# Attention and feed-forward on one core: values of batch 0 on ScalarE's DMA queue, the first weight's transfers ahead of the second's, other constants for the planned order

## The chip, the cores and the metric

The kernel runs on one core of a Trainium2 chip. Its engines are TensorE (PE, matrix products), VectorE (DVE), ScalarE (ACT), GpSimd (POOL) and SyncE (SP, which here only issues DMAs). The metric is the device time of one execution in microseconds (us). The kernel before took 361.05 us, the median of three runs (359.9 to 361.69).

## The reference

Causal attention with 16 extra "beacon" keys and values in front, for 8 batches, 8 heads, 576 rows and 64 dimensions; then a feed-forward layer with an ELU between its two products, on 4608 tokens of 512 features with 2048 hidden ones.

```python
k_all = concatenate([beacon_k, k], axis=2)
v_all = concatenate([beacon_v, v], axis=2)
scores = (1 / sqrt(D)) * matmul(q, k_all^T)
scores = where(causal, -1e9, scores)
a = exp(scores - scores.max(-1)); a /= a.sum(-1) + 1e-9
attn = matmul(a, v_all)
x = attn.transpose(0, 2, 1, 3).reshape(B * S, H * D)
h = x @ w_in
g = where(h > 0, h, exp(min(h, 0)) - 1)
out = g @ w_out
```

## The kernel before

The heads of a batch are worked on in four pairs (`HP = 4`; pair n is batch n // 4, pair n % 4 in it). One pair goes through these steps:

- load of k and q (`load_pair`, L310) into one `st` buffer of four, cast to bf16 (`cast_pair`, L317 and L319), transposes on PE and copies out of PSUM to `kT` and `qT` (`do_T2` and `do_copy2` for batch 0, L394 to L411; `do_T`, `do_kT`, `do_qT` for batches 1 and 2, L384 to L426). From batch 3 on (`PE_B = 3`) tokens are loaded whole (`load_tok`) and transposed by DMA (`turn_tok`, L349).
- scores (`do_SC`, L435), exponentials on ACT (`do_exp`, L444), causal masks on POOL (`do_mask`, L450), the product with the values (`do_AV`, L469; the value tile has a column of ones, so the sum of the row comes with it), the division (`do_norm`, L484 and L485, DVE), and the transposes of the result into `xT` (`do_xT`, `do_xcopy`, L495 and L506, or by DMA, `turn_x`, L355). Batch 0 does this in three ranges of query rows, and a range needs the chunks of values that its rows can see.

The values of a batch come in five chunks of 128 keys (`load_v`, L361 for the 16 beacon rows of the first chunk and L365). Chunk jc of batch b has the name v(5b + jc): v0 to v4 are batch 0, v5 to v9 batch 1. They land in four buffers called `vst`, which the beacon keys (b0, b1, b2) use too, and are cast by DVE (`cast_v`, L369).

The feed-forward layer takes the tokens in tiles: 128, 128, 256 and then 512 rows. `do_mm1` (L522) makes hidden values in PSUM, `do_e` (L528, ACT) their exponential, `do_clamp` (L532, POOL) and `do_join` (L541, DVE) the ELU, `do_mm2` (L549) the second product, `do_osb` and `do_store` (L555, L559) the output. Its two weights come in four chunks each on POOL's queue (`load_w`, L376).

Nothing here is in the order in which it is written. Each step is added to a `Plan` with an engine, a key, an estimated duration, the steps it depends on and the buffers it takes and gives; `Plan.run` plays this through as a list scheduler while the program is built: whenever an engine is free it takes the ready step with the smallest key, and the instructions are then written out in that order, which each engine follows on the chip. On PE a step whose key is more than 16 above the smallest one not yet done is not taken. While the plan's time is below 30 and PE has nothing ready, it writes `spare` matmuls (`do_fill`, L272). The keys come from the constants at L563 to L577:

- `SHIFT` and `AT`: a step of batch b has the key `32 * (b - 1) + 8 * (hp + AT[i]) + SHIFT[b]`; `AT0` gives the keys of batch 0's scores, for three ranges and four pairs. `URGE` is taken off the keys of copies and divisions.
- `PACES` and `LAG`: the keys of the feed-forward tiles.
- `FIRST`: the order of the first loads, ahead of every other load. k0, q0 and b0 come before them.
- `W_AFTER`: for each of the four chunks of the two weights, the number of the mark after which it is issued. The marks are the masks of batches 0 and 1 and the first beacon cast, sorted by key; negative numbers mean the first mark.
- `ON_ACT`: whether token loads of k, of q, and value loads (of batches 3 and up) are issued by ACT; otherwise SP issues them. `ON_POOL` says which engine casts pair n (0 DVE, 1 POOL, 2 ACT), `TOK` the same for tokens, `Q_ON_ACT` and `X_ON_ACT` which batch's copies ACT does.

Loads on the same queue are issued in the order of their keys. ACT's loads stand in the same instruction stream as its exponentials.

Of the kernel before, what the change touches and what calls it, by code (L numbers as in the profile page):

```python
# [26 lines left out]
class Plan:  # L27
# [5 lines left out]
    def add(self, *args, **kw):  # L33
        op = Op(*args, **kw)
        self.ops.append(op)
        return op
# [102 lines left out]
def kernel(  # L139
# [87 lines left out]
    PE_B = 3  # L227
# [32 lines left out]
    with tc.tile_pool(name="psum", bufs=1, space=bass.MemoryType.PSUM) as psum:  # L260
# [21 lines left out]
        def load(key, dur, fn, deps=(), take=(), issue=0.47, units=1, on="SP"):  # L282
            ring = ["ring" + on] * units
            issue = add(on, key, issue, fn, deps=deps, take=take + ring)
            issues[on].append(issue)
            if "vst" not in take:
                issues["st"].append(issue)
            return add("DMA", key, dur, None, deps=[issue], lat=2.0, give=ring, queue=0 if on == "SP" else 2, parts=2 * units)

        issues = {"SP": [], "ACT": [], "st": []}  # L290
        add("SP", -1e6, 0.8, None)
        add("PE", -1e6, 1.3, None, mode=0)
# [264 lines left out]
        def do_store(tt, t4):  # L557
# [2 lines left out]

        SHIFT = [26.52, -13.69, -7.54, -1.34, 6.61, 17.9, 20.31, 13.93]  # L563
        AT = [-45.47, -1.07, -1.14, -0.54, -0.28, 0.56, 0.84, -22.77]
        AT0 = [[-37.75, -28.54, -33.52, -38.24], [-24.55, -26.86, -32.24, -21.75], [-25.0, -22.71, -32.03, -23.64]]
        PACES = [(-23.75, 5.53, 18.69, 9.14), (4.36, -4.25, 29.71, 6.23), (-11.12, 1.43, 43.67, -1.88), (36.29, 0.26, 8.05, 3.71), (81.1, 1.29, 17.28, 1.76), (112.87, 2.15, 30.1, 2.15)]
        W_AFTER = [[-11.34, -130.29, -36.3, -85.47], [23.62, 2.53, 18.3, 19.29]]
        DMA_AT = [-71.28, -109.08, 210.39]
        TOK = ("010110", "101001", "110100", "111111", "101001")
        ON_POOL = "11000121"  # L570
        X_ON_ACT = "00"
        LAG = 20.54
        URGE = 125.33
        Q_ON_ACT = "11001010"
        FIRST = (
            "v1 k2 q2 q3 k1 v2 q4 k3 q1 v0 v4 v3 k4 q6 b1 q5 v6 q7 k6 k5 v5 v8 k7 v9 v7 ").split()
        ON_ACT = "011"  # L577

        def place(b, a):
            return 32 * (b - 1) + 8 * a + SHIFT[b]  # L580

# [6 lines left out]
        def load_key(name, key):  # L588
            return ["k0", "q0", "b0"].index(name) - 900 if name in ("k0", "q0", "b0") else FIRST.index(name) - 200 if name in FIRST else key
# [3 lines left out]
        def plan_loads(n):  # L593
# [8 lines left out]
            for is_k in (True, False):  # L602
# [3 lines left out]
                "0": ("DVE", 0.9, nc.vector), "1": ("POOL", 1.23, nc.gpsimd), "2": ("ACT", 1.35, nc.scalar),  # L606
            }[ON_POOL[n] if n < len(ON_POOL) else "1"]
            qk_in[n] = add(
                eng, place(b, hp + AT[0]), dur, partial(cast_pair, n, on), deps=gots + [last_T.get(("pair", n - 2))], take=["sb"], give=["st"])

        last_T = {}

        def plan_v(b):
            for jc in range(NKC):
                key = load_key(f"v{NKC * b + jc}", place(b - 1, 1.8 + 0.4 * jc))
                on, eng = QUEUES[ON_ACT[2] == "1" and b >= PE_B]
                got = load(key, 1.22, partial(load_v, b, jc, eng), take=["vst"], issue=1.2 if jc == 0 else 0.6, units=8, on=on)
                v_cast[b, jc] = add(
                    "DVE", place(b, -0.7 + 0.16 * jc), 0.56, partial(cast_v, b, jc),
                    deps=[got] + last_AV.get(b - 2, []), give=["vst"])  # L620

        def plan_w(which, f4):
            after = marks[max(0, min(len(marks) - 1, round(W_AFTER[which][f4])))]
            got = add("POOL", after.key + 0.01, 0.8, partial(load_w, which, f4), deps=[after])
            got = add("DMA", 0, 3.2, None, deps=[got], lat=2.0, queue=1, parts=8)
            w_at.update({(which, 4 * f4 + c): got for c in range(4)})
# [3 lines left out]
        ring4, QUEUES = ["ringSP"] * 4, (("SP", nc.sync), ("ACT", nc.scalar))  # L630

        def plan_tok(b):
            turned[b] = []
            for is_k in (True, False):
                for c in range(0, NKC, 2):
                    m = min(2, NKC - c)
                    i = (0 if is_k else 0.5) + c // 2
                    on, eng = QUEUES[ON_ACT[not is_k] == "1"]
                    gots = [load(place(b, 0) - 30 + i + 0.01 * j, 1.22, partial(load_tok, b, is_k, c + j, eng), units=8, on=on,
                                 take=["st"] if j == 0 else [], issue=1.2 if is_k and c + j == 0 else 0.65) for j in range(m)]  # L640
                    on_dve = TOK[b - PE_B][3 * (not is_k) + c // 2] == "0"
                    cast = add("DVE" if on_dve else "POOL", place(b, DMA_AT[0]) + i, 0.36 * m if on_dve else 0.53 * m,
                               partial(cast_tok, b, is_k, c, m, nc.vector if on_dve else nc.gpsimd),
                               deps=gots, take=["sb"], give=["st"])
                    for j in range(m):
                        s = add("SP", place(b, DMA_AT[1]) + i, 1.25, partial(turn_tok, b, is_k, c + j),
                                deps=[cast] + last_SC.get(b - 2, []), take=ring4)
                        turned[b].append(add("DMA", place(b, DMA_AT[1]) + i, 0.6, None, deps=[s],
                                             give=ring4 + (["sb"] if j == m - 1 else []), lat=1.9, parts=8))

        def plan_T2(n, key):
            b, hp = divmod(n, HP)
            T = last_T["pair", n] = add(
                "PE", key, 0.56, partial(do_T2, n), deps=[qk_in[n], bk_in[b]], take=["ff", "ff"], give=["sb"],
                mode=0, lat=0.19)
            last_T.setdefault(b, []).append(T)
            kA = add("DVE", key + 0.4 - URGE, 0.47, partial(do_copy2, n, 0, 0, nc.vector), deps=[T])
            qB = add("ACT", key + 0.4 - URGE, 0.4, partial(do_copy2, n, 1, 1, nc.scalar), deps=[T])
            qA = add("ACT", key + 0.5 - URGE, 0.45, partial(do_copy2, n, 1, 0, nc.scalar), deps=[kA])
            kB = add("DVE", key + 0.5 - URGE, 0.57, partial(do_copy2, n, 0, 1, nc.vector), deps=[qB])  # L660
            add("NONE", key, 0.0, None, deps=[kA, qA], give=["ff"], lat=0.0)
            add("NONE", key, 0.0, None, deps=[kB, qB], give=["ff"], lat=0.0)
            return [kA, kB, qA, qB]

        def plan_T(n, key):
# [5 lines left out]
            last_T["pair", n] = T  # L671
            kT = add("DVE", key + 0.4 - URGE, 0.92, partial(do_kT, n), deps=[T, last_kq.get(n - NKQ)])
            if Q_ON_ACT[b] == "1":
                qT = add("ACT", key + 0.4 - URGE, 0.7, partial(do_qT, n, nc.scalar), deps=[kT, last_kq.get(n - NKQ)])
            else:
# [4 lines left out]
        def plan_pair(n):  # L680
            b, hp = divmod(n, HP)
            at = lambda a: place(b, hp + a)
            key = AT0[0][hp] - 4 if b == 0 else at(AT[1])
            ready = plan_T2(n, key) if b == 0 else plan_T(n, key) if b < PE_B else turned[b]
            masked = {}
            SC = None
            steps = [((0,), AT0[0][hp]), ((1, 2), AT0[1][hp]), ((3,), AT0[2][hp])] if b == 0 else \
                [((0, 1), at(AT[2])), ((2, 3), at(AT[3]))]
            for units, key in steps:
# [19 lines left out]
            for r, groups in enumerate([(0,), (1,), (2,)] if b == 0 else [(0,), (1, 2)]):  # L709
                key = AT0[r][hp] + 2.4 if b == 0 else at(AT[4 + r])  # L710
                us = [u for g in groups for u in CUT.of_range[g]]
# [9 lines left out]
                if b >= XB:  # L721
                    for blk in blks:
                        part.setdefault(blk, []).append(normed[-1])
                    if hp == HP - 1:
                        for blk in blks:
                            s = add("SP", at(AT[7]), 1.25, partial(turn_x, b, blk), deps=part.pop(blk), take=ring4)
                            done = add("DMA", at(AT[7]), 0.6, None, deps=[s], give=ring4, lat=1.9, parts=8)
                            last_X.setdefault(b, []).append(done)
# [13 lines left out]
                normed = []  # L742
                on_act = X_ON_ACT[b] == "1"
                done = add("ACT" if on_act else "DVE", key - URGE, 0.17 + 0.00104 * w if on_act else 0.15 + w / 1920,
# [6 lines left out]
        def plan_tile(p):  # L751
            lo, hi = TILES[p]
            base, pitch1, start2, pitch2 = PACES[p] if p < len(PACES) else (32 * (p - 2) + LAG,) + PACES[-1][1:]
            xs = []
# [45 lines left out]
        for b in range(B):  # L800
            plan_v(b)
            if b >= PE_B:
                plan_tok(b)
            for hp in range(HP):
                if b < PE_B:
                    plan_loads(b * HP + hp)
                plan_pair(b * HP + hp)
# [40 lines left out]
```

## Time and profile before

The page of the profiled execution gives the span from the first to the last instruction and the busy time of each engine.

| what | us |
|---|---|
| median of three runs | 361.05 |
| the profiled execution | 360.17 |
| its span | 358.5 |
| PE busy, `spare` among it | 344.4 |
| `spare` matmuls (117) | 19.1 |
| L522 and L549, the feed-forward products | 143.1 and 143.8 |
| scores and A·V (L435, L469) | 35.2 and 40.1 |
| DVE, ACT, POOL busy | 205.1, 192.7, 183.8 |

The granted clock of PE is at full speed nearly throughout (mean 0.998). The DMA engines are at nine tenths or more in most of the slices up to 250 us. In the listing of waits, a line "A <- B: t, n, longest" says that A's engine stood t us in n waits which B ended. In the timeline each row is a start, a length, the engine, the line, the operation and its tiles; "q" behind an engine's name is its queue of DMA issues. In the table of stretches, busy time is the time in which at least one instruction of the engine was under way.

### The profile page before, as it was taken

To read this page: it belongs to the slowest core of one execution; us is meant where nothing else is said; L and a number is where in the kernel's file an instruction comes from. 1 tells how busy PE (TensorE), PEld (TensorE's weight loads), DVE (VectorE), ACT (ScalarE), POOL (GpSimd) and SP (SyncE) were. 2 spreads that over 40 slices of the span, in tenths; PEclk is the share of its full clock that TensorE was granted. 3 is DMA by queue.
4 is the path that set the end of the run, shared out by engine and by line. 5 is a ranking of instruction groups with operands and counts; after the bars stand their busy time and mean duration, and the time that the engine had idled before them with its cause. 6 is when DMAs were issued, how large, how long until landed. Compare 5 with 4: busy or idle time off the path is not lost.

```text
span 358.5 us, 8337 instructions
## 1 busy us (share of the span) xinstructions
PE 344.4 (96%) x3221; PEld 187.1 (52%) x3221; DVE 205.1 (57%) x424; ACT 192.7 (54%) x286; POOL 183.8 (51%) x359
## 2 busy tenths in 40 slices
PE   8999989997998999999999999899999999999995
PEld 5767876554454543545455545455555444444442
DVE  3377777765663757646835476567455555545421
ACT  2687885465745745764876447555863333333200
POOL 5567876356723745753675556454654343343200
PEclk9999999999999999999999999999999999999999
DMA  7999995694999998999797999999102310000022
GB/s 231 252 287 217 197 250 138 187 210 105 178 163 242 144 144 182 207 224 175 145 196 165 138 188 185 187 172 170 40 31 57 89 39 30 31 30 29 31 93 82
DMA packets 139335, 52.53 MB, mean 147 GB/s; under 512 B 127520, under 2 KB 131616, under 8 KB 139296
## 3 DMA queue, kind: packets, MB, share of 16 engines
q1 hardware_dynamic: 87328, 35.55, 47.4%
q10 hardware_dynamic: 47744, 12.26, 20.3%
q0 software_dynamic: 4224, 4.19, 7.0%
q8 instruction: 25, 0.41, 0.5%
q14 instruction: 14, 0.11, 0.1%
HBM read 37.22 MB, written 9.44 MB: 130 GB/s over the span
## 4 chain that ended last, share of the span: by engine, by line
PE 75%; DMA 10%; DVE 3%; POOL 3%; issue 3%; SPq 3%; ACT 1%; ACTq 0%; POOLq 0%
PE ops L549 30%; PE hps L522 28%; PE sc L435 6%; PE av L469 6%; DMA st<-in_k_dram 5%; PE spare L272 2%; DMA w_in<-in_moe_w_in_dram 2%; SPq L355 2%; DVE gt L541 1%; POOL e L532 1%; DMA qT<-st 1%; DMA st<-in_q_dram 1%; POOL et L450 1%; PE tr L384 1%; DVE v L369 1%
## 5 line engine op out<-in xcount | busy, mean ns | idle before, releaser
L522 PE MATMUL hps<-xT,w_in 128*128 128x512 f16 (+2 forms) x704 | 143.1, 340 | 4.9 <-DVE gt L541 3.8
L549 PE MATMUL ops<-w_out,gt 128*128 128x512 f16 x576 | 143.8, 379 | 0.8 <-DVE gt L541 0.8
L541 DVE SCALAR_TENSOR_TENSOR gt<-e,hps 128x512 f16<-128x512 f32 x144 | 97.2, 684 | 78.0 <-POOL e L532 77.8
L532 POOL TENSOR_SCALAR e<-e 128x512 f32<-128x512 f32 x144 | 89.4, 624 | 92.6 <-ACT e L528 92.3
L528 ACT ACTIVATE e<-hps 128x512 f32<-128x512 f32 x144 | 85.5, 599 | 95.4 <-PE hps L522 85.5
L444 ACT ACTIVATE et<-sc 128x768 f16<-128x768 f32 (+3 forms) x128 | 104.6, 863 | 40.8 <-PE sc L435 30.2
L522 PEld LDWEIGHTS <-w_in 128*128 128x128 f16 x704 | 60.5, 98 | 61.3 <-issue 6.6
L549 PEld LDWEIGHTS <-gt 128*128 128x128 f16 x576 | 53.2, 98 | 61.8 <-issue 3.4
L450 POOL TENSOR_SCALAR_AFFINE_SELECT et<-et 128x256 f16<-128x256 f16 (+2 forms) x160 | 59.8, 401 | 44.1 <-ACT et L444 42.2
L469 PEld LDWEIGHTS <-et 128*128 128x128 f16 (+1 forms) x960 | 35.9, 97 | 12.6 <-issue 2.2
L469 PE MATMUL av<-v,et 128*128 128x65 f16 (+1 forms) x960 | 40.1, 193 | 1.3 <-POOL et L450 1.2
L555 DVE COPY osb<-ops 128x512 f32<-128x512 f32 x36 | 24.8, 689 | 27.6 <-PE ops L549 27.3
L435 PE MATMUL sc<-qT,kT 64*128 64x80 bf16 (+3 forms) x704 | 35.2, 228 | 1.3 <-ACT qT L424 1.0
L485 DVE TENSOR_TENSOR x<-av,rl 128x256 f16<-128x256 f32 (+2 forms) x68 | 32.1, 471 | 2.3
L435 PEld LDWEIGHTS <-kT 64*128 64x128 bf16 x704 | 20.8, 95 | 23.1 <-issue 21.2
L369 DVE CAST v<-vst 128x512 f16<-128x512 f32 (+1 forms) x40 | 21.2, 533 | 6.3 <-DMA vst<-in_v_dram 6.3
L484 DVE RECIPROCAL rl<-av 128x4 f32<-128x4 f32 (+2 forms) x68 | 12.4, 183 | 20.3 <-PE av L469 19.5
L342 POOL CAST st<-st 128x1024 bf16<-128x1024 f32 (+2 forms) x18 | 16.1, 892 | 15.1 <-DMA kT<-st 3.7
L272 PE MATMUL spare<-ones 128*128 128x256 bf16 x117 | 19.1, 295 | 1.7 <-DVE ones L790 1.3
L272 PEld LDWEIGHTS <-ones 128*128 128x128 bf16 x117 | 11.4, 105 | 5.9 <-DVE ones L790 1.3
L342 DVE CAST st<-st 128x1024 bf16<-128x1024 f32 (+2 forms) x12 | 8.2, 682 | 5.9 <-DMA st<-in_q_dram 5.2
L319 POOL CAST st<-st 128x1152 bf16<-128x1152 f32 x8 | 9.1, 1142 | 1.5 <-DMA st<-in_q_dram 1.5
(37 smaller groups left out, 68.5 us busy)
## 6 DMA issues: line engine op xcount, KB each, us to landing
out_dram<-osb SPq DMA_DIRECT2D x36, 256.0 KB, 2.2
st<-in_q_dram ACTq DMA_DIRECT2D x20, 256.0 KB, 4.7
st<-in_k_dram SPq DMA_DIRECT2D x15, 256.0 KB, 5.3
vst<-in_v_dram ACTq DMA_DIRECT2D x15, 256.0 KB, 4.1
st<-in_k_dram SPq DMA_DIRECT2D x12, 288.0 KB, 5.4
st<-in_q_dram SPq DMA_DIRECT2D x11, 288.0 KB, 5.4
vst<-in_v_dram SPq DMA_DIRECT2D x9, 256.0 KB, 4.5
w_out<-in_moe_w_out_dram POOLq DMA_DIRECT2D x4, 512.0 KB, 14.1
```

What stands on the lines that cost most here:

```text
L272: nc.tensor.matmul(out=spare[:, 0:2 * P], lhsT=ones[:, 0:P], rhs=ones, start=True, stop=True)
L435: nc.tensor.matmul(out=sc[:, h, o:o + w], lhsT=kT[D * h:D * h + D, P * jc:P * jc + P], rhs=qT[D * h:D * h + D, q0:q0 + w], start=True, sto ...
L444: nc.scalar.activation(out=et[:, :, 0:w], in_=scs[n, u][:, :, 0:w], func=AFT.Exp, bias=0.0, scale=float(1.0 / (D ** 0.5)))
L450: nc.gpsimd.affine_select(out=et[:, :, c0:c0 + dw], in_=et[:, :, c0:c0 + dw], compare_op=ALU.is_ge, fill=fill0, base=q0 + NB - P * jc, pat ...
L469: nc.tensor.matmul(out=av[:, c:c + D + 1], lhsT=ets[n, CUT.unit_of[jc, at]][0:m, h, col:col + P], rhs=v16[0:m, jc, 2 * hp + h, 0:D + 1], s ...
L485: nc.vector.tensor_tensor(out=x16s[b % 2][:, blks[0]:blks[0] + nb, P * hp:P * hp + P].rearrange("q i (h d) -> q i h d", d=D), in0=av[:, :, ...
L522: nc.tensor.matmul(out=hps[:, (hi - lo) * j:(hi - lo) * (j + 1)], lhsT=w_in16[:, cc, P * fc:P * fc + P], rhs=xT[cc][:, lo:hi], start=(cc = ...
L528: nc.scalar.activation(out=e, in_=hpss[tt, i], func=AFT.Exp, bias=0.0, scale=1.0)
L532: nc.gpsimd.tensor_scalar(out=e, in0=e, scalar1=1.0, scalar2=0.0, op0=ALU.min, op1=ALU.max)
L541: nc.vector.scalar_tensor_tensor(out=gt, in0=es[tt, i], scalar=1.0, in1=hpss[tt, i], op0=ALU.subtract, op1=ALU.max)
L549: nc.tensor.matmul(out=ops, lhsT=gts[tt, fc][:, P * t4:P * (t4 + 1)], rhs=w_out16[:, fc, :], start=(fc == 0), stop=(fc == NFC - 1))
L555: nc.vector.tensor_copy(out=osb, in_=opss[tt, t4])
```

## The change

Values get a queue for each batch: `V_ON_ACT[b]` says whether ACT issues them. Batch 0 and batches 3 to 6 are "1", batches 1, 2 and 7 "0"; before, batches 3 to 7 were on ACT. As a batch's values can now be on another queue than those of the batch ahead, they also depend on that batch's issues, from batch 2 on. All constants of the order are others. Among them: in `FIRST` the pairs of batch 0 come in the order 0, 2, 1, 3 (before 0, 2, 3, 1), v9 is among the first loads, and k4 comes later; all four chunks of the first weight stay tied to the first mark, which is now a mask of pair 1, and the chunks of the second are tied to marks 21, 26, 27 and 28 (before 24, 3, 18 and 19); `URGE` is negative; `ON_POOL` gives the cast of pair 0 to DVE (before POOL), of pair 3 to POOL (before DVE), of pair 4 to ACT (before DVE) and of pair 6 to POOL (before ACT); `Q_ON_ACT` gives batch 2's q copies to ACT; `X_ON_ACT` gives batch 1's copies of the transposed result to ACT.

```diff
+        v_issue = {}
         issues = {"SP": [], "ACT": [], "st": []}
...
-        SHIFT = [26.52, -13.69, -7.54, -1.34, 6.61, 17.9, 20.31, 13.93]
-        AT = [-45.47, -1.07, -1.14, -0.54, -0.28, 0.56, 0.84, -22.77]
-        AT0 = [[-37.75, -28.54, -33.52, -38.24], [-24.55, -26.86, -32.24, -21.75], [-25.0, -22.71, -32.03, -23.64]]
-        PACES = [(-23.75, 5.53, 18.69, 9.14), (4.36, -4.25, 29.71, 6.23), (-11.12, 1.43, 43.67, -1.88), (36.29, 0.26, 8.05, 3.71), (81.1, 1.29, 17.28, 1.76), (112.87, 2.15, 30.1, 2.15)]
-        W_AFTER = [[-11.34, -130.29, -36.3, -85.47], [23.62, 2.53, 18.3, 19.29]]
-        DMA_AT = [-71.28, -109.08, 210.39]
-        TOK = ("010110", "101001", "110100", "111111", "101001")
-        ON_POOL = "11000121"
-        X_ON_ACT = "00"
-        LAG = 20.54
-        URGE = 125.33
-        Q_ON_ACT = "11001010"
+        SHIFT = [9.39, -11.99, 3.16, -1.24, 2.1, 8.36, 21.51, 15.8]
+        AT = [-48.95, -1.97, -0.92, 0.07, 0.3, 1.11, 2.63, -12.35]
+        AT0 = [[-43.3, -48.0, -45.55, -30.15], [-37.72, -30.95, -32.36, -14.21], [-44.52, -28.42, -32.66, -26.9]]
+        PACES = [(-22.47, 1.13, 13.54, 7.42), (-6.86, 4.46, 39.22, 0.86), (-11.1, 1.86, 32.62, 3.87), (31.04, 1.25, 3.9, 3.25), (68.13, 1.29, 18.34, 3.13), (107.16, 2.11, 30.72, 2.1)]
+        W_AFTER = [[-52.07, -83.73, -134.26, -263.01], [21.44, 26.5, 27.22, 27.88]]
+        DMA_AT = [-187.37, -171.67, 236.92]
+        TOK = ("000111", "110111", "011110", "001000", "101100")
+        ON_POOL = "01012111"
+        X_ON_ACT = "01"
+        LAG = 22.19
+        URGE = -106.49
+        Q_ON_ACT = "11111110"
         FIRST = (
-            "v1 k2 q2 q3 k1 v2 q4 k3 q1 v0 v4 v3 k4 q6 b1 q5 v6 q7 k6 k5 v5 v8 k7 v9 v7 ").split()
-        ON_ACT = "011"
+            "v1 k2 q2 k1 v9 q1 v0 k3 q3 q6 v3 v8 v6 q5 v2 q4 v4 k4 b1 k5 k7 k6 v7 v5 q7 ").split()
+        ON_ACT = "01"
+        V_ON_ACT = "10011110"
...
-                on, eng = QUEUES[ON_ACT[2] == "1" and b >= PE_B]
-                got = load(key, 1.22, partial(load_v, b, jc, eng), take=["vst"], issue=1.2 if jc == 0 else 0.6, units=8, on=on)
+                on, eng = QUEUES[V_ON_ACT[b] == "1"]
+                got = load(key, 1.22, partial(load_v, b, jc, eng), take=["vst"], issue=1.2 if jc == 0 else 0.6, units=8, on=on,
+                           deps=v_issue[b - 1] if b > 1 else ())
+                v_issue.setdefault(b, []).append(issues[on][-1])
```

## The prediction

> **What bounds the kernel now.** First the table of ten stretches, for the share of TensorE (PE), then its `spare` matmuls, which do nothing but keep it running while it has no work.
>
> ```profile
> 0.00:10.00 10.00, 8.45 (x63) 6.02 (x64) 2.93 (x10) 2.85 (x4) 4.71 (x20) 1.00 0.80 238
> 10.00:20.00 10.00, 9.95 (x111) 7.09 (x109) 4.87 (x13) 6.67 (x13) 4.83 (x9) 1.00 1.20 265
> 20.00:30.00 10.00, 9.84 (x194) 7.11 (x193) 7.49 (x30) 7.89 (x11) 8.76 (x17) 1.00 1.13 252
> 30.00:40.00 10.00, 9.28 (x148) 8.18 (x145) 7.21 (x21) 8.09 (x14) 6.96 (x14) 1.00 1.21 212
> ```
>
> Columns: stretch, length, busy us of PE, PE weight loads, DVE, ACT and POOL with counts, granted clock, DMA share, GB/s. PE looks full from 1 us on, and it isn't. The same stretches for `spare` alone:
>
> ```profile
> 0.00:10.00 10.00, 7.55 (x44) 1.00 0.80 238
> 10.00:20.00 10.00, 7.44 (x52) 1.00 1.20 265
> 20.00:25.00 5.00, 2.61 (x16) 1.00 0.99 291
> 25.00:32.00 7.00, 1.55 (x8) 1.00 1.24 228
> ```
>
> So of the first 32 us 19.15 are filler, and 2.4 are idle (25 - 23.41 = 1.59 up to 25 us, 7 - 6.17 = 0.83 after). PE's useful work up to 32 us is about 10.5 us. Later it is nearly the bound itself: idle 26 - 24.57 = 1.4 us in 32 to 58, 82 - 77.36 = 4.6 in 58 to 140, 100 - 98.29 = 1.7 in 140 to 240, nothing in 240 to 340, and 3.85 in the tail. What can be won lies in the start, then in the 6.3 us between 58 and 240.
>
> Third, the chain of waits in order of time, and the timelines of PE, DVE and SP's queue, for what the start waits for.
>
> ```profile
> 22.70 0.87 POOL et L450 x2
> 23.57 8.43 DMA w_in<-in_moe_w_in_dram
> 32.05 1.07 PE hps L522 x16
> ```
> ```profile
> 20.49 0.54 PE L469 MATMUL av<-v,et 128*128 128x65 f16 x12
> ```
> ```profile
> 19.10 0.75 DVE L369 CAST v<-vst 128x512 f16<-128x512 f32 x2
> ```
> ```profile
> 8.37 0.59 SPq L361 DMA_DIRECT2D vst<-in_beacon_v_dram  x1
> ```
>
> Read from the last row up: v0, which every A·V product needs, is put on SP's queue only from 8.37 us, behind eleven loads; it is cast in the pair of casts at 19.10, and the first A·V (L469) runs at 20.49, though the first masked tile was there at 10.83. The first weight is asked for at 23.57, behind a mask (L450), lands at 32.00, and the first hidden-layer matmul (L522) starts at 32.05.
>
> **The change, part by part.**
>
> *Values of batch 0 on ScalarE's queue.* Six issues (five chunks and the beacon rows) of 0.4 to 0.6 us leave SP's queue, some 3 us of it, and go to ACT's. ACT waits 5.18 us for its first copy at 7.26, with its table load over at 2.1: v1 and v0 (three issues, 0.44 + 0.59 + 0.42) fit there and cost nothing; without that idle time they would hold up the copy by 1.5 us. v0 is then issued by 3.7 us; with the 6.1 us that value loads take to land (median of the stretch) and a cast of 0.5 it is there at 10.3 instead of 19.5. A·V costs about 0.035 us a matmul (24 in 0.84 us in the chain), so 120 x 0.035 = 4.2 us for the batch, and its transposes some 1.3 us more. Up to 25 us only 38 of the 120 (1.3 us) and 0.4 us of transposes had run, so 3.8 us of useful work could change places with filler. Ends: 0 (ScalarE's exponentials, 14 us for the batch, set the pace and not v0) and 3.8. I take 2.0: pairs 0 and 2 have their exponentials done by 16.3 us, that is half of the batch.
>
> The other three loads (v3, v2, v4) fall where ACT is two thirds busy: 1.5 us of issues against 20 - 6.67 - 7.89 = 5.4 us of idle time between 10 and 30. I charge 0.3 us; ends 0 and 1.5.
>
> *First weight ahead.* All four chunks of w_in are tied, before and after, to the first mask by key. That was pair 3's (key -37.44); it is pair 1's now (-48 + 0.8), whose k1 and q1 are third in the list of loads. The third pair's transposes came at 15.47 before, its copies end about 17.1, then scores 0.33, exponential 0.78, masks 0.74: issue at about 19.0, ends 16 and 20, against 23.57. With the 8.43 us of the first chunk the first L522 comes at 27.5. Between 25 and 32 us there is 1.55 us of filler and 0.83 of idle, so at most 2.4 us to fill, at least 0; the chunks come one after the other, so I take half, 1.2. The four issues hold POOL for 3.53 us; at 19 they fall in its wait of 4.03 us before 20.73. With that cover gone, masks wait 3.5 us. The chunk of w_out that was at 10.83 moves behind.
>
> *Casts.* Pair 0's cast goes from POOL (1.14 us, on the chain at 5.25) to DVE (0.76): 0.4 earlier for all that follows; the beacon cast of 0.60 must also be done, so I take 0.3 (ends 0 and 0.4). Pair 3's goes the other way, 0.4 later, under the exponentials of the pairs ahead of it; without those the 0.3 are gone.
>
> *Other constants.* The four q copies of batch 2 go from DVE (0.75 each) to ACT (0.65); ACT is busy 46.0 of the 82 us from 58 to 140, so nothing; without that room it is 2.6 us. Batch 1's four copies of the transposed result go from DVE to ACT too; no row has that on ACT, so by the nearest, the q copy of the same 576 columns (0.65; the one of 256 columns, 0.46, is the low end), 2.6 us, where ACT is busy 19.62 of 26 us (32 to 58): nothing, or 2.6 if no gap fits. The casts of pairs 4 and 6 trade places between ACT and the others, one on ACT as before. Batch 7's values go to SP, six issues of 0.4 to 0.6 us: SP's longest wait is for outputs (82 us in all), so nothing. The sign of URGE turns: copies and normalisations (DVE, ACT) now go behind a join that is ready at the same time, 0.68 us a time. All places in the order past batch 2 change; the trace does not say which way. What is there to win is the 6.3 us of idle; as bounds I take 3 us of gain (half of it) and 6 us of loss (as much again), and zero as the value, for the seven waits that make up the 6.3 us (0.3 to 1.95 us each: on joins, one on a mask, one on an exponential) have no common cause that the change names.
>
> *Sum.* 2.0 + 1.2 + 0.3 - 0.3 = 3.2 us. The profiled run has 360.17 us (span 358.5, 1.67 around it), 0.88 below the median of the three: 357.0 on its terms, **357.9** against the median 361.05.
>
> **Rivals.**
>
> *A, the forecast:* 357.9, its own range 355.5 to 359.3.
>
> *B, the transfers hold the start.* The DMA share is 1.1 to 1.2 from 10 to 50 us, so v0 early means k or q late, and nothing is won but issue time: 361.05. For it: loads of k and q took 4.7 to 5.0 us in the first 7 us and 7.0 to 7.3 between 14 and 24, beside one chunk of w_out. Against it: the same eight k and q loads and one or two values stand ahead of the last pair in both lists, so the order and not the amount changes. The Trainium skill, "DMA: Bandwidth & Descriptors", section "Issuing engines are not separate DMA queues", says that a second issuing engine saves only the time of the issue; by it the sum would be about 0, and no row here shows it, as batch 0 used one queue for values.
>
> *C, given back at the second weight.* Chunks 1 to 3 of w_out now hang on masks of batch 1's pair 1 (keys -10.55 and -2.63). If they land after 56 us, TensorE, ahead by 3.2 us, runs dry of other work: first L549 at 53.91 before, behind 0.99 us of idle. 361.0. Against it: chunk 0, the last one before (issued 40.57), is now the first.
>
> *D, slower: ScalarE's queue stands still.* A load that finds no free buffer of the four `vst` blocks every exponential behind it.
>
> ```profile
> ACT e L528 <- DMA vst<-in_beacon_v_dram: 3.0, 1, 3.0
> ```
>
> That is what one such load cost at 128 us, and it was in the chain. Users of the four buffers are now b0, v1, v9, v0, v3, v8, v6, v2, v4: v3 waits for b0's cast, v2 for v0's, v4 for v3's, in the stretch where ACT feeds everything. Two stands of 3.0 us: 357.9 + 6.0 = 363.9. It decides from 3.2 us of standing in all. Against it: with v0 cast at 10.3 a buffer is free early.
>
> *E, the later waits shrink too:* 357.9 - 3 = 354.9.
>
> **How the numbers follow.** A 0.45, B 0.10, C 0.11, D 0.28, E 0.06. No change means within 0.5% (1.8 us, 359.25 to 362.85), about what a measurement of this kernel can tell. Faster: 0.41 of A, E, 0.02 each of B and C = 0.51. Same: 0.04 of A, 0.06 each of B and C, 0.01 of D = 0.17. Slower: the rest, 0.32, nearly all D, and in it the loss of up to 6 us in later stretches. The range reaches from E's 354.9, rounded down, to just past D: 354.5 to 364.5; A alone 355.5 to 359.3.
>
> **What would show it.** Right: first A·V near 11 us, first L522 at 26 to 29, filler below 16 us in the first 32, idle between 58 and 240 near 6.3. Wrong: the first A·V still at 20 (B); a new idle stretch of PE between 48 and 58 with w_out as its end (C); ACT waiting more than 3 us on `vst` before 32 us (D); idle in 58 to 240 above 9 us, which no term of the sum covers.

## The result, and the profile after

| | median us | lowest to highest | ratio to before (95%) |
|---|---|---|---|
| before, 20 runs beside it | 361.40 | 359.68 to 362.28 | |
| after, 20 runs | 364.34 | 361.08 to 367.19 | 1.0082 (1.0059 to 1.0105) |

The kernel became slower by 0.8%, about 3 us. Medians here are of all executions, and ratios leave out those more than 1.5% above the fastest of their kernel. The profiled execution took 364.66, with a span of 362.9, 4.4 more than before. So the question is why 3.2 us of forecast gain became 3 us of loss, a distance of some 6 us.

First the table of stretches of the changed kernel, all engines (columns as in the prediction), then for `spare` alone.

```profile
0.00:10.00 10.00, 4.79 (x30) 3.54 (x31) 1.76 (x7) 1.28 (x1) 3.63 (x19) 0.88 0.88 229
10.00:20.00 10.00, 9.95 (x101) 6.88 (x99) 4.45 (x13) 5.64 (x9) 3.06 (x7) 0.78 0.76 205
20.00:30.00 10.00, 9.72 (x144) 6.44 (x143) 7.33 (x24) 7.40 (x12) 8.07 (x15) 1.00 0.92 223
30.00:40.00 10.00, 9.86 (x178) 8.32 (x176) 6.80 (x27) 7.69 (x10) 7.24 (x14) 1.00 1.21 211
```
```profile
0.00:10.00 10.00, 4.07 (x23) 0.88 0.88 229
10.00:20.00 10.00, 7.45 (x41) 0.78 0.76 205
20.00:25.00 5.00, 3.18 (x20) 1.00 0.85 237
25.00:32.00 7.00, 3.22 (x15) 1.00 1.03 224
```

In the first 10 us PE is busy 4.79 us where it was 8.45, in 30 instructions where there were 63. In the next 10 it looks as full as before, but at a granted clock of 0.78: 101 instructions take the time that 111 took. The DMA share is lower too, 0.76 for 1.20. So the loss begins in the first 20 us, ahead of the first A·V and of the first weight, on which the two largest terms of the forecast were built. Line numbers from here on are one higher than before (L394 is L395), and in later kernels they move by the lines that an edit adds.

What PE waited for, and what that waited for, in the timelines of PE, DVE and ACT's queue of the changed kernel:

```profile
1.26 4.07 PE L272 MATMUL spare<-ones 128*128 128x256 bf16 x23 [1.26 <-DVE ones L794]
9.29 1.14 PE L395 MATMUL tr<-identb,st 128*128 128x128 bf16 x9 [3.96 <-DVE st L320]
10.33 2.56 PE L272 MATMUL spare<-ones 128*128 128x256 bf16 x11
14.45 0.67 PE L395 MATMUL tr<-identb,st 128*128 128x128 bf16 x9
17.02 0.35 PE L470 MATMUL av<-v,et 128*128 128x65 f16 x6
34.80 1.05 PE L523 MATMUL hps<-xT,w_in 128*128 128x128 f16 x16
```
```profile
8.47 0.76 DVE L320 CAST st<-st 128x1152 bf16<-128x1152 f32 x1 [6.87 <-DMA st<-in_q_dram]
```
```profile
0.84 0.43 ACTq L366 DMA_DIRECT2D vst<-in_v_dram  x1
1.30 0.60 ACTq L362 DMA_DIRECT2D vst<-in_beacon_v_dram  x1
1.93 0.45 ACTq L366 DMA_DIRECT2D vst<-in_v_dram  x1
2.42 0.69 ACTq L311 DMA_DIRECT2D st<-in_q_dram  x1
```

And ACT's queue of the kernel before:

```profile
0.84 0.75 ACTq L310 DMA_DIRECT2D st<-in_q_dram  x1
```

Read from the last fence up. q0 is ACT's, in both kernels: `load_pair` writes the q load of pair 0 with `nc.scalar`, in a line that the change does not touch, while the plan holds it for a load of SP's queue. Before, ACT had nothing else to issue and q0 went out at 0.84. Now the planner gives ACT three value loads that are ready at once, and q0 is written behind them: out at 2.42. The chain of waits of the changed kernel begins with it:

```profile
2.42 5.96 DMA st<-in_q_dram
9.29 1.14 PE tr L395 x9
```

In the kernel before, the chain and the cast in it were:

```profile
0.84 4.28 DMA st<-in_q_dram
5.25 1.15 POOL st L319
6.45 0.68 PE tr L394 x9
```

The transfer takes 5.96 us; before it took 4.28. With 1.58 us of later issue and 1.68 us of longer transfer, the first cast starts at 8.47 for 5.25, and PE, whose filler is written out in a fixed number, stands for 3.96 us ahead of its first transposes. The clock is at 0.50 from 8 to 14 us, and the eleven fillers at 10.33 take 2.56 us. In the kernel before, at full clock, eleven took 1.68:

```profile
10.30 1.68 PE L272 MATMUL spare<-ones 128*128 128x256 bf16 x11
```

### The profile page after: what moved, and what is told of

Same layout as the page of the kernel before. It is cut to its first block, busy times and chain, and to the rows that moved or that the text cites. A ratio compares the mean times of both kernels' runs of the same rounds, so it can differ in the third digit from the quotient of the medians.

```text
span 362.9 us, 8322 instructions
## 1 busy us (share of the span) xinstructions
PE 345.9 (95%) x3208; PEld 187.1 (52%) x3208; DVE 200.5 (55%) x417; ACT 196.9 (54%) x294; POOL 182.1 (50%) x358
## 4 chain that ended last, share of the span: by engine, by line
PE 85%; DMA 7%; POOL 2%; DVE 2%; issue 2%; ACT 1%; ACTq 1%; SPq 0%; POOLq 0%; DVEq 0%
PE hps L523 34%; PE ops L550 31%; PE av L470 8%; PE sc L436 7%; DMA st<-in_q_dram 5%; PE spare L272 4%; DMA xT<-x 1%; PE tr L385 1%; POOL et L451 1%; DMA out_dram<-osb 1%; DVE gt L542 1%; PE tr L395 1%; POOL e L533 1%; DVE x L486 1%; PE xt L496 0%
## 5 line engine op out<-in xcount | busy, mean ns | idle before, releaser
L533 POOL TENSOR_SCALAR e<-e 128x512 f32<-128x512 f32 x144 | 88.2, 616 | 98.5 <-ACT e L529 97.6
L445 ACT ACTIVATE et<-sc 128x736 f16<-128x736 f32 (+3 forms) x128 | 104.2, 863 | 33.2 <-PE sc L436 28.4
L523 PEld LDWEIGHTS <-w_in 128*128 128x128 f16 x704 | 61.4, 98 | 64.4 <-issue 6.8
L451 POOL TENSOR_SCALAR_AFFINE_SELECT et<-et 128x256 f16<-128x256 f16 (+2 forms) x160 | 60.6, 403 | 48.0 <-ACT et L445 45.3
L343 POOL CAST st<-st 128x1024 bf16<-128x1024 f32 (+2 forms) x16 | 14.4, 901 | 10.1 <-DMA st<-in_q_dram 3.0
L370 DVE CAST v<-vst 128x512 f16<-128x512 f32 (+1 forms) x40 | 18.9, 486 | 0.5 <-DMA vst<-in_v_dram 0.5
L272 PEld LDWEIGHTS <-ones 128*128 128x128 bf16 x104 | 10.4, 110 | 6.5 <-issue 2.3
L343 DVE CAST st<-st 128x1024 bf16<-128x1024 f32 (+2 forms) x14 | 10.2, 726 | 5.1 <-DMA st<-in_beacon_k_dram 2.2
L320 POOL CAST st<-st 128x1152 bf16<-128x1152 f32 x9 | 10.3, 1140 | 0.0
```

What stands on the lines that cost most here:

```text
L272: nc.tensor.matmul(out=spare[:, 0:2 * P], lhsT=ones[:, 0:P], rhs=ones, start=True, stop=True)
L445: nc.scalar.activation(out=et[:, :, 0:w], in_=scs[n, u][:, :, 0:w], func=AFT.Exp, bias=0.0, scale=float(1.0 / (D ** 0.5)))
L451: nc.gpsimd.affine_select(out=et[:, :, c0:c0 + dw], in_=et[:, :, c0:c0 + dw], compare_op=ALU.is_ge, fill=fill0, base=q0 + NB - P * jc, pat ...
L523: nc.tensor.matmul(out=hps[:, (hi - lo) * j:(hi - lo) * (j + 1)], lhsT=w_in16[:, cc, P * fc:P * fc + P], rhs=xT[cc][:, lo:hi], start=(cc = ...
L533: nc.gpsimd.tensor_scalar(out=e, in0=e, scalar1=1.0, scalar2=0.0, op0=ALU.min, op1=ALU.max)
```

## The experiments

The theory from this reading: q0 is late and everything behind it follows; the rest of the change is worth about what the forecast said. Rivals: the values on ACT's queue, or the other constants, are themselves what costs; the slow clock and not the late load costs the time; the place of the first weight does. All ratios are to runs of the kernel before on the same chip, with 95% intervals.

### q0 first again

After, with one load written to ACT ahead of all others:

```diff
+            if n == 0 and not is_k:
+                if ahead:
+                    return
+                ahead.append(n)
...
+        load_pair(0, False)
         plan.run()
```

> The changed kernel with one thing moved: q0 is written to ScalarE's queue ahead of v1, the beacon rows and v0 instead of behind them; the order of everything else stays. Theory 1 (q0 behind three value loads delays the whole head by 3.2 us, 8.47 against 5.25 for the first cast, and TensorE's wait of 3.96 us halves its clock until 14.5 us): first cast back at about 5.2, no idle time of TensorE before 25 us beyond 1.6 us, time 360.0 to 361.3. Theory 2 (the loss is made later, at 113 to 116, 167 to 174 and 227 us, and what the head loses is taken up by slack before 58 us): 363.3 to 364.5.

358.74 (357.17 to 360.84, 12 runs), ratio 0.9941 (0.9917 to 0.9965). Its timeline of PE, with lines 6 higher than after:

```profile
6.16 0.96 PE L401 MATMUL tr<-identb,st 128*128 128x128 bf16 x9
9.96 0.68 PE L401 MATMUL tr<-identb,st 128*128 128x128 bf16 x9
12.53 0.35 PE L476 MATMUL av<-v,et 128*128 128x65 f16 x6
30.32 1.05 PE L529 MATMUL hps<-xT,w_in 128*128 128x128 f16 x16
```

Against the same rows of after: 3.13 us earlier at the first transposes, 4.49 at the second pair's, 4.49 at the first A·V, 4.48 at the first hidden product, and 5.0 in the span (357.9 for 362.9). By the ratios the place of this one load is worth 0.0141 x 361.4 = 5.1 us (3.9 to 6.3 with the spread of both). It is the cause of the loss, and with q0 first the kernel is faster than both. The time is below the 360.0 to 361.3 that were expected.

### The same in the old order

The kernel before, with v1, the beacon rows and v0 written to ACT ahead of everything, q0 too:

```diff
+        load_v(0, 1, nc.scalar)
+        load_v(0, 0, nc.scalar)
         plan.run()
```

> The kernel before with v1, the beacon rows and v0 written to ScalarE's queue ahead of q0; nothing else is changed. Theory 1: the first cast comes 3.2 us later than in the kernel before, TensorE's clock falls before 14 us, time 364 to 365.5 (3.2 us less up to 1 that the early v0 gives back, plus up to 1 of slow clock). Theory 2: 361 to 362.5.

The same with q0 ahead of the three:

```diff
+        load_pair(0, False)
+        load_v(0, 1, nc.scalar)
+        load_v(0, 0, nc.scalar)
         plan.run()
```

> The kernel before with v1, the beacon rows and v0 on ScalarE's queue right behind q0; nothing else is changed. The first term of the predicted sum by itself, in the old order. As predicted (v0's lateness is what the first A·V waits for, 2.0 us): 358.9 to 360.0. Rival (the order of TensorE's work is fixed while the program is built, and the old order has the first A·V late whatever v0 does; so nothing is won): 360.6 to 362, first A·V still near 20 us.

Values ahead of q0: 368.62 (364.61 to 369.85, 6 runs), ratio 1.0175 (1.0128 to 1.0221). Values behind it: 362.93 (361.0 to 366.15, 12 runs), ratio 1.0045 (1.0018 to 1.0073). The two differ in the place of q0 alone: 1.3%, 4.7 us, without any of the changed constants. Both times are above all that was expected of them. The first one's timeline of PE:

```profile
9.70 0.68 PE L400 MATMUL tr<-identb,st 128*128 128x128 bf16 x9 [3.74 <-POOL st L319]
37.42 0.79 PE L528 MATMUL hps<-xT,w_in 128*128 128x128 f16 x11 [1.47 <-DMA w_in<-in_moe_w_in_dram]
```

The first transposes come 3.25 us later than before (6.45), the first hidden product 5.37 us later (32.05). The second kernel says something of the forecast's first term: v0 early in an order that does not use it is no gain but a loss of 0.45%. Its first A·V ran at 22.47, no earlier than 20.49, and the cast of pair 2 at 9.89 for 8.31.

The first of the two was looked at once more.

> The kernel before with v1 and v0 ahead of q0 (368.62) once more for its profile, as the one taken was the fastest of its six (364.61). Theory 1: the first cast comes at 8.5 again and the 4 us between 364.6 and 368.6 lie in waits behind 58 us. Rival: q0's transfer itself varies from run to run (first cast anywhere from 8 to 12 us), and the time with it.

368.09, with the first cast at 8.96 (8.50 in the first look) and the first hidden product at 37.31. Its distance to before is 5.3 us at 59 us, 5.0 at 92 and 7.9 at 238, behind waits of PE of 2.01 us at 121 and 1.41 at 145. The first profiled execution, 364.61, is at the same place at 92 us (92.15 for 92.12) and ended only 4.4 us behind before. So q0's delay varies little, and the 3.5 us between these two executions of one kernel come from 121 us and later.

### Which of it: the place in the queue, or the shared transfer

After, with q0 on SP's queue, as the plan has it:

```diff
-            eng = nc.scalar if n == 0 and not is_k else nc.sync
+            eng = nc.sync
```

> The changed kernel with q0 written to SP's queue, where the plan has it (second, behind k0), and v1 and v0 left first on ScalarE's queue. It parts the two halves of q0's delay: the later issue (1.58 us) and the longer transfer (5.96 against 4.28 us, behind v1 and v0 in the same row of DMA work). Theory 1a (its place in ScalarE's queue is the whole of it): issue at 1.6, first cast at 5.9 to 6.3, time 358.8 to 360.3. Theory 1b (v1 and v0 take the transfer time from q0 on any queue): first cast at 7 or later, time 361 to 363.

360.79 (358.97 to 363.11, 12 runs), ratio 0.9982 (0.9952 to 1.0012), in the middle. Its timeline of DVE:

```profile
7.54 0.76 DVE L320 CAST st<-st 128x1152 bf16<-128x1152 f32 x1 [5.94 <-DMA st<-in_q_dram]
```

The cast is 0.93 us earlier than in after and 2.2 later than with q0 first (5.34). q0 now goes out at about 1.6, 0.82 us earlier than in after, but its transfer still takes some 6 us: v1 and v0, on another engine's queue, go out at the same time. That q0 now stands behind k0 on SP's queue is new too, and the two were not tried apart. Of the 3.13 us by which the cast is late in after, then, 1.58 are the later issue and the rest the longer transfer, and this run takes back half of the first and little of the second. Of the time it takes back more, 3.6 us of 5.1: the wait of PE is 2.6 us instead of 3.96, and the clock of the first 25 us 0.93 instead of 0.86. Against the kernel with q0 first, transposes that start 2.2 us late cost only 1.5 us here. The time lies between the two forecasts.

### The clock

After, with 36 and with 24 more fillers ahead of the first transposes, so that PE does not stand:

```diff
+            for _ in range(36 if n == 0 else 0):
+                do_fill()
             trs[n] = [...]
```

> The changed kernel with 36 more filler matmuls in front of the first transposes, so that TensorE doesn't stop before its first data; q0 stays late. It prices the clock alone. Theory 1: clock at full speed from 0 to 25 us, first cast still at 8.5, time 363.3 to 364.0, that is 0.4 to 1.0 us less than the changed kernel, and less spread between runs. Theory 2 (the clock costs nothing, or the fillers get in the way): no difference or slower, 364.3 to 365.

> The changed kernel with 24 more filler matmuls in front of the first transposes (36 in the run before of this kind, whose times lay too far apart to tell). What the halved clock costs: at half speed the planned fillers between the first and the second pair's transposes take twice as long, and TensorE takes them in order. Theory 1: clock at 0.95 or more from 8 to 15 us, second pair's transposes 1.2 to 1.8 us earlier than 14.45, median 362 to 363.5. Rival (the start is 1.7 us earlier and later waits take it back): the start moves as said, median 364 to 365.5.

365.09 (362.38 to 370.55, 6 runs), ratio 1.0120 (1.0069 to 1.0170), and 364.17 (362.63 to 365.58, 6 runs), ratio 1.0104 (1.0068 to 1.0139). The stretch from 8 to 15 us, first of after, then with 36 fillers:

```profile
8.00:15.00 7.00, 5.71 (x41) 3.95 (x41) 2.83 (x7) 1.55 (x3) 0.80 (x3) 0.54 0.99 277
```
```profile
8.00:15.00 7.00, 6.95 (x73) 5.14 (x71) 4.20 (x10) 2.99 (x6) 1.83 (x3) 1.00 0.97 279
```

The clock is full and the second pair's transposes come at 12.80 and 13.07 instead of 14.45; the first hidden product at 33.13 and 33.39 instead of 34.80. So the half clock explains why a delay of 3.1 us became 4.5, though fillers take 1.5 times as long under it (2.56 for 1.68 us) and not twice as expected. But the end is not shown to be earlier in either. With 24 fillers the profiled execution is 1.4 us ahead of after's up to 92 us and 4.1 at 160, and most of it is gone at one wait, in its timeline of PE:

```profile
166.33 1.87 PE L552 MATMUL ops<-w_out,gt 128*128 128x512 f16 x4 [3.43 <-DVE gt L544]
```

The rival that the clock costs the time is not borne out. The times with 36 fillers lie so far apart (362.4 to 370.6; the four below 366 have a median of 364.3) that a gain of 1.5 us could be hidden in them.

### A late head with q0's transfer left alone

Pair 0's cast repeated on the same data, three times more on POOL in the kernel before, four times more on DVE in the one with q0 first:

```diff
+            for _ in range(3 if n == 0 else 0):
+                eng.tensor_copy(out=dst, in_=src)
```

> The kernel before, with pair 0's cast done four times over (three extra casts of 1.14 us on POOL, 3.4 us in all); every transfer is issued as before. A late head without late transfers. Theory 1 (the kernel simply shifts by what its head is late): 361.3 + 3.4 = 364.7, within 1. Rival A (late transfers, not the late cast, make up what q0's delay costs beyond 3.2 us): 362 to 363.7. Rival B (the late head itself is paid twice, as the order behind it is fixed for an earlier one): 366 to 369.

> The run with q0 first (358.74), with four extra casts of 0.76 us on DVE ahead of pair 0's (3.0 us); transfers as there. The same question in the new order. Theory 1: 358.7 + 3.0 = 361.7, within 1. Rival A: 359 to 360.7. Rival B: 363 to 365, as slow as the changed kernel.

365.61 (363.78 to 366.65, 4 runs), ratio 1.0148 (1.0093 to 1.0202); and 362.19 (359.65 to 365.06, 10 runs), ratio 1.0049 (1.0014 to 1.0083), 1.08% above the kernel it is made from. The first one's timeline of PE:

```profile
10.30 1.14 PE L396 MATMUL tr<-identb,st 128*128 128x128 bf16 x9 [3.67 <-POOL st L321]
38.75 1.07 PE L524 MATMUL hps<-xT,w_in 128*128 128x128 f16 x16 [1.57 <-DMA w_in<-in_moe_w_in_dram]
```

3.85 us at the first transposes are 6.7 at the first hidden product and 5.3 in the time (3.4 to 7.3). In the new order the four casts take 3.43 us, the first transposes come 3.54 us later (9.70), and the time is 3.9 us longer (2.4 to 5.4 with the spread of both). Only the loads ahead of the first cast go out as before. Those behind it move, unlike what was expected: SP's next load of q goes out when the cast has freed a buffer, here in the old order, late and before:

```profile
10.27 0.60 SPq L310 DMA_DIRECT2D st<-in_q_dram  x1
```
```profile
6.42 0.61 SPq L310 DMA_DIRECT2D st<-in_q_dram  x1
```

So a head that is late by its cast alone, with q0's transfer as it was, costs about its own lateness. That it costs more is not clear of the spread in these two, and what the later loads have in it was not tried apart.

### The values on the other queue

The kernel with q0 first, its values of batch 0 on SP's queue in the planned place (k0, q0 and the beacon keys written first):

```diff
+            if b == 0:
+                eng = nc.sync
...
+        load_pair(0, True)
+        load_pair(0, False)
+        load_bk(0)
         plan.run()
```

> The changed kernel with q0 first, as in the run before, and batch 0's five chunks of values on SP's queue in the place that the plan gave them (v1 and v0 right behind b0, v3 to v4 among k and q). What ScalarE's queue is worth for these loads, with the order the same. Theory 1 (the queue as such is worth little; only what stands ahead of q0 counts): k2 and q2 are issued 1.5 us later, pair 2's cast is 0 to 1 us later, time within 1.2 us of the run before. Theory 2 (the second queue is what buys the early values): over 2 us slower than the run before.

360.22 (359.05 to 362.23, 12 runs), ratio 0.9970 (0.9945 to 0.9994): 1.5 us above the kernel with q0 first by the medians, 1.0 by the ratios. The first A·V runs at 12.91 instead of 12.53. So what the change is named for is worth little, and v0 is early because of its place in the list of loads, not because of the engine that issues it. The Trainium skill, "DMA: Bandwidth & Descriptors", section "Issuing engines are not separate DMA queues", says that a second issuing engine saves only the time of the issue; the rows do not speak against it: without ACT's queue k2 goes out at 4.11 instead of 2.23, and 0.4 us of that are left at the first A·V.

Then v0 and the beacon rows on SP behind q2, v1 on ACT:

```diff
+            if n == 2 and not is_k:
+                load_v(0, 0, nc.sync)
```

> The run with q0 first (358.74), with v0 and its beacon rows on SP's queue behind k2 and q2, so that they no longer share the transfers with q0, k2 and q2; v1, v3, v2 and v4 stay on ScalarE's queue. If sharing the transfers is what delays pair 2's cast (9.14 against 8.31 in the kernel before): cast of pair 2 at 8.2 to 8.7, time 357.8 to 358.9. Rival (k1 and q1 are then late by as much): 358.7 to 360.

358.91 (356.19 to 365.78, 12 runs), ratio 0.9941 (0.9913 to 0.9969), the same as with q0 first. The cast of pair 2, at 9.14 there, came no earlier for it, at 9.04. Once q0 is ahead, the place of v0 within these few loads makes no difference that shows.

### The first weight

With q0 first, the four issues of w_in held back and written behind pair 3's first masks, nothing else moved:

```diff
+            if which == 0 and len(late) < 4:
+                late.append(f4)
+                return
...
+            if (n, u, jc) == (3, 0, 1):
+                for f4 in list(late):
+                    load_w(0, f4)
```

> The run with q0 first (358.74), with the four issues of the first weight written behind pair 3's first masks on POOL's queue instead of pair 1's; no other place changes, unlike in the run that planned anew. The second term of the predicted sum (1.2 us) undone, cleanly. As predicted: issue at 25 instead of 20, first L522 at 33 to 34 instead of 30.3, time 359.5 to 361. Rival (TensorE has enough to do until then, so the place is hidden): 358.2 to 359.2. Rival (the fixed order stops at the first L522, all of it is lost): 361.5 to 363.

361.16 (358.62 to 365.23, 12 runs), ratio 1.0009 (0.9975 to 1.0042). The issue moves from 19.96 to 27.0, the first hidden product from 30.32 to 33.48, and 0.68% is lost, 2.4 us (0.9 to 4.0 with the spread of both): the early weight is worth that much in this order, where 1.2 were forecast. That the time is longer rests on the ratio alone. Between the two profiled executions the 3.16 us are 2.7 at 152 us and gone behind 163, where the one with q0 first waits:

```profile
163.15 1.27 PE L556 MATMUL ops<-w_out,gt 128*128 128x512 f16 x4 [2.96 <-DVE gt L548]
```

In the kernel before, the same four issues written earlier, behind pair 2's first masks:

```diff
+            if (n, u, jc) == (2, 0, 1):
+                for f4 in range(4):
+                    load_w(0, f4)
```

> The kernel before with the four issues of the first weight written behind pair 2's first masks (about 14 us) instead of pair 3's (23.6); all else in its place. The second term by itself in the old order. As predicted: first L522 at about 31.3, its wait of 0.72 us gone, 360.3 to 361.2. Rival (in the fixed old order nothing is ready to use it, and the transfers of k, q and v beside it come late): 361.5 to 364.

365.45 (364.69 to 368.12, 6 runs), ratio 1.0159 (1.0118 to 1.0199). Its timelines of POOL and PE:

```profile
14.55 2.99 POOL L381 DMA_DIRECT2D w_in<-in_moe_w_in_dram  x4
17.51 1.19 POOL L319 CAST st<-st 128x1152 bf16<-128x1152 f32 x1
```
```profile
18.75 0.68 PE L399 MATMUL tr<-identb,st 128*128 128x128 bf16 x9 [2.98 <-POOL st L319]
```

Here the cover is gone that the prediction named for POOL's issues, only that a cast and not a mask stands behind them: the cast of pair 1 waits until 17.51 (14.16 before), PE stands 2.98 us and runs at half clock for some 3 us soon after, and the first hidden product, its weight long asked for, comes at 35.70 for 32.05. The transfers that the rival names are slower too: three loads of k and q issued between 11 and 17 us take 11.8 and 12.7 us by their medians, 7.2 and 8.9 before. The two were not parted, and the time is above both forecasts.

### Two plans made anew

After, with the plan told that q0 is on ACT's queue; and the kernel with q0 first, its weight tied to the old marks:

```diff
+                                 on="SP" if n or is_k else "ACT"))
```
```diff
-        W_AFTER = [[-52.07, -83.73, -134.26, -263.01], [21.44, 26.5, 27.22, 27.88]]
+        W_AFTER = [[15, 15, 15, 15], [24, 0, 18, 19]]
```

> The changed kernel with q0's load planned on ScalarE's queue, where it is written, so that the plan puts it first; the order of all else is planned anew with the same constants. Theory 1: first cast at 5.3, time within 1.5 us of the run with q0 moved by hand (358.74), 357.5 to 360.2. Rival (a new plan moves later waits about by more than that): outside it, either way.

> The run with q0 first (358.74), with the first weight's four chunks tied to a mask of pair 3 and one chunk of the second weight ahead of them, as in the kernel before. The second term of the predicted sum undone (1.2 us). As predicted: w_in issued 4 to 6 us later, first L522 near 35, time 359.5 to 361. Rival (TensorE has batch 0's work until 31 us anyway, the first weight's place is hidden): 358.2 to 359.2.

375.84 (374.42 to 376.85, 6 runs), ratio 1.0394 (1.0360 to 1.0427), although the first cast starts at 5.29; and 373.43 (370.93 to 376.01, 6 runs), ratio 1.0330 (1.0289 to 1.0371). Both failed to show what they were made for. Each edit lets the list scheduler make the whole order again, with constants that were set for another one, and new waits of PE appear in many places: in the first 2.59 us at 24 us and 2.52 at 142, in the second 2.86 at 124 and 5.11 at 172. That is why the other experiments move single issues without a new plan.

## Why the prediction was wrong, and what of it held

**The step that failed** is in the first term: "v1 and v0 (three issues, 0.44 + 0.59 + 0.42) fit there and cost nothing". The idle time of the engine was looked at, and not what already stood in its queue. q0 was there at 0.84, the only row of ACT's queue at the start, and the chain of waits named that load as its first transfer. The forecast had v0 issued by 3.7 us, and with q0 first it goes out at 3.11; in after it goes out at 1.93, ahead of q0. The three issues put ahead of q0 cost not 0 but 5.1 us. The working followed the values off SP's queue and asked of ACT only whether it had time; the load that they were put in front of has no term in the sum.

**How 3.1 us become 5.** Up to the second pair's transposes the kernels with more filler show it: 3.1 us of delay, and 1.4 more because the transposes and the written fillers run at half clock. Most of the lateness then stays: the rows of after stand 4.49 us behind those of the kernel with q0 first at the first output product (51.08 for 46.59), 3.7 from 54 us on, as the kernel with q0 first waits 0.66 us for w_out, and 5.05 at a wait on a transfer, here in the timeline of after and then of the other:

```profile
116.48 4.44 PE L523 MATMUL hps<-xT,w_in 128*128 128x512 f16 x12 [2.88 <-DMA xT<-x]
```

```profile
111.43 2.75 PE L529 MATMUL hps<-xT,w_in 128*128 128x512 f16 x12 [1.66 <-DMA xT<-x]
```

Behind it after is 6.7 us late, as its twelve products run at half clock; behind 163 us, where the kernel with q0 first waits 2.96 us, it is 3.0 late, and at the end 5.0. PE is nearly the bound from 32 us on, so little of a late head can be made good. The loads are dragged along: SP's queue stands behind two loads of q until the casts of values at 16.10 free a buffer, and between 14 and 16 us the DMA engines, at 1.20 with q0 first, are at 0.04. SP's queue in after:

```profile
8.02 1.84 SPq L311 DMA_DIRECT2D st<-in_q_dram  x2
16.55 1.04 SPq L366 DMA_DIRECT2D vst<-in_v_dram  x2
```

and with q0 first, where the same two value loads go out 4.48 us sooner:

```profile
9.34 1.32 SPq L317 DMA_DIRECT2D st<-in_q_dram  x2
12.07 1.04 SPq L372 DMA_DIRECT2D vst<-in_v_dram  x2
```

So the 5.0 us of these two executions are the 4.49 of the head and what the later waits take and give. Why those differ so much between executions (after spreads over 6.1 us, the kernel with 36 fillers over 8.2, the kernel before over 2.6 to 4.1) stays open.

**The other terms.** With q0 first the kernel takes 358.74, by the ratio 2.1 us less than before (1.3 to 3.0), where 3.2 were forecast. The sum was a third too large, and its parts were off both ways:

- The values' term (+2.0): 1.0 to 1.5 for the queue, and no gain in the old order (a loss of 0.45%). The charge for the other three values was not measured by itself. The first A·V came at 12.53, not near 11. It was to replace filler, and filler did not fall below 16 us: 19.56 with q0 first, 19.15 before. So what was won did not come this way.
- The first weight (+1.2): 2.4 (0.9 to 4.0). Its issue was forecast for 19.0 and is at 19.96, the first hidden product for 27.5 and is at 30.32, out of the 26 to 29 named for it. The first chunk landed 8.8 us after its issue, at 28.8, and PE came to the product without a wait, so the order of PE's work set this time and not the weight. After has 24.47 and 34.80, both out of their ranges.
- Pair 0's cast on DVE (+0.3): the transposes start 6.16 for 6.45. Right.
- The other constants (0): idle time of PE between 58 and 240 us is 6.92 in after and 5.99 with q0 first, where 6.3 was named. Right for that stretch. The terms that were measured by themselves add up to some 4 us against 2.1, but each has a spread of 1 us or more, so it is not shown that the constants take something back; that was not tried.

**The rivals.** D gave 363.9 from two stands of ACT's queue on `vst`. The time is close and the mechanism another. Its sign did show: behind q0's issue, over at 3.11, ACT's next value load goes out only when POOL's cast of the beacon keys has freed a buffer, 3.6 us later. Rows of after:

```profile
6.07 0.60 POOL L303 CAST bk<-bk 16x512 bf16<-16x512 f32 x1 [2.29 <-DMA bk<-in_beacon_k_dram]
```
```profile
6.70 0.39 ACTq L366 DMA_DIRECT2D vst<-in_v_dram  x1
```

But no exponential was ready then: ACT's first copy comes at 10.57, and it waited for PE. The long stand was SP's, until 16.55. B, by which v0 early means k or q late, has its part: q0's transfer grew by 1.68 us next to v1's and v0's. C did not show in after; with q0 first, PE waits 0.66 us on w_out at 50.77, a small part of it. E did not show: the later waits are 6.92 and 5.99 us, not 3.

## What to carry to other kernels

Before a load is moved to an idle engine's queue, look up what is already issued there, and whether the planner's queue for it is the one that the code writes: three issues of half a microsecond ahead of the first load of the chain cost 5 us. In a kernel whose bound engine follows a fixed order and has little slack later, lateness at the start is paid for, though not at a fixed rate (2.2 us at the first transposes cost 1.5, and 3.1 to 3.9 cost 3.9 to 5.3). Constants that were set for one planned order say nothing of another; test a part by moving single issues in an order that is kept.

## What was not expected of the hardware

A wait of 3.96 us left PE at a granted clock of 0.50 for 6.8 us, although it was kept busy from 9.29 on. The Trainium skill, "TensorE: Matmul & The Clock Gate", section "Why this matters for your kernels", asks for no gaps above some 3 us between matmuls; the row at 9.29 agrees. In these traces all ten waits of PE of 2.9 us and more were followed by such a stretch, and seven of the twenty between 1.7 and 2.9 us: the wait of 2.88 us ahead of the twelve matmuls at 116.48 was (they take 4.44 us, and 2.75 in the kernel with q0 first), and one of 2.86 us in the second plan made anew was not. The clock can also fall late. Behind the wait of 2.98 us with the early weight in the old order the transposes at 18.75 still take their usual 0.68, and then the table of stretches has 0.50:

```profile
20.00:23.00 3.00, 3.00 (x23) 2.11 (x23) 0.99 (x3) 0.62 (x2) 0.00 (x0) 0.50 1.17 260
```

Apart from the ends of the programs, each slow stretch lasted 3.4 or 6.8 us, nothing in between.

And one 5.96 us transfer for 4.28: in the traces of after and of the kernel with q0 on SP's queue, q0's transfer takes some 6 us alike, whether three value loads stand ahead of it on its own queue or go out on another engine's at the same time.
